# Attention batch 0 whole before the feed-forward part, and half of the k/q transposes by DMA: one change to an attention plus ReGLU kernel

## The chip, the cores and the metric

One core of a Trainium2 chip. The metric is the device time of one execution in microseconds (us), median over repeated runs; 95% intervals use runs in the fast state alone. A "span" is the time from the first to the last instruction of a profiled execution; it is about 1.8 us shorter than the time of the same run. "Clock" is the mean TensorE clock that the profile shows as granted, 1.0 being full speed; below it is the mean over a whole span unless a window is named. In the profiles PE is TensorE (PEld its weight loads), DVE VectorE, ACT ScalarE, POOL GpSimd and SP SyncE, which here only issues DMAs; a q behind a name, as in SPq, stands for the issuing itself. PSUM is the memory that the matmuls write.

## The reference, cut to what matters

```python
# q, k, v: (4 batches, 8 heads, 768 rows, 64); n_sink = 4, window = 128
scores = q @ k.T / 8                              # per batch and head
keep   = (key < 4) | (0 <= query - key < 128)     # 4 sink keys and a sliding window
a      = softmax(where(keep, scores, -1e9))
x      = (a @ v) -> (3072 tokens, 512)
out    = (relu(x @ w_gate) * (x @ w_val)) @ w_out # 512 -> 1536 -> 512
```

The comparison allows bf16 arithmetic. All three weight matrices are fp32 in memory and are cast to bf16 by the DMA that loads them.

## The kernel before: the parts that matter

Two heads are attended together, which I call a unit: 4 units per batch, 16 in all. A unit is a row of stages: `S(0)`, `S(1)`, `S(2)` (scores of three groups of queries, then exp), `T` (transposes of the *next* unit's k and q), and two `norm` (sums and outputs `V`, then the division). The feed-forward part is a row of 96 "chunks": 384 tokens by 128 of the 1536 columns, with gp and vp (four matmuls each), and op matmuls (the output product) some chunks later. Stages are woven between chunks by a plan.

```python
# batch 0 is attended in two halves: units of kind "L" (rows 0 to 375), then "M" (the rest)
U  = [Unit(p, 0, p, "L") for p in range(NP)] + [Unit(NP + p, 0, p, "M") for p in range(NP)]
U += [Unit(2 * NP + (b - 1) * NP + p, b, p, "F") for b in range(1, B) for p in range(NP)]

def T(self, pool, shape, tag, qcopy=nc.scalar.copy):        # every unit: TensorE, then two ScalarE copies
    # ... cut
    for t in range(kn_):
        nc.tensor.transpose(ps[:, t * kp:(t + 1) * kp], self.kn_[0:kp, t, :, :]..., ident[0:kp, 0:kp])
    # ... cut: the same for q, copies PSUM -> kT, qT, and the small copies that place the sink keys (kTs)

# head: four half units, before the first chunk
for p in range(NP):
    U[p].S(0)
    # ... cut: casts and loads
    U[p].S(1)
    if p + 2 < NP:
        U[p + 2].T(*GV)
    # ... cut: loads of weights and casts
    warm(8)                                                  # matmuls on the identity, no useful work
    if p >= 1:
        norm(U[p - 1], 0, ps_gv)
# ... cut
ORDER  = [(0, h, m) for h, m in [(h, m) for h in range(2) for m in range(FM)]]   # token half, then weight column
ORDER += [(b, h, m) for b in range(1, B) for h in range(2) for m in range(FM)]
PLAN = ((0, 0), (2, 0), (10, 19), (23, 43), (47, 67), (71, 89), (72, 90))        # (chunk, stages done by then)
```

The softmax here doesn't subtract the row's maximum and nothing guards it: scores larger than these inputs give would overflow.

## Time and profile before

| | before |
|---|---|
| time, median of 3 runs | 276.72 us (275.81 to 277.87) |
| span of the profiled run | 273.9 us, at clock 0.999 |
| TensorE busy | 259.8 us (95%) |
| first full chunk | 22.8 us |

TensorE is the bound; how that is read, with the page's lines, stands in the prediction below. On the page, the line of all packets and the line of DMA queue q1, which carries all loads that SP (SyncE) issues (columns: packets, megabytes, share of the 16 DMA engines' span):

```profile
DMA packets 46858, 31.20 MB, mean 114 GB/s; under 512 B 28400, under 2 KB 43760, under 8 KB 46832
q1 hardware_dynamic: 40224, 25.93, 34.2%
```

And one row of the table of windows, from 10 to 20 us: busy time and count for each engine, granted clock, DMA share, GB/s.

```profile
10.00:20.00 10.00, 9.87 (x131) 6.61 (x130) 6.63 (x15) 6.57 (x14) 8.29 (x18) 1.00 1.23 234
```

### The profile page before, as it was taken

Reading aid. Unit: us, or ns where it says so; the run is one execution under the profiler, and the core shown is the slowest. Engines: PE = TensorE matmul, PEld = TensorE weight load, DVE = VectorE, ACT = ScalarE, POOL = GpSimd, SP = SyncE. Lnnn points to the kernel's source line nnn. Section 1 sums busy time; section 2 is a strip of 40 time slices with the busy share of each in tenths; the row PEclk is TensorE's granted clock in tenths of the full one; section 3 lists DMA queues with packets and bytes.
Section 4 is the critical chain, followed back from the end, with each engine's and each line's share of the span. In section 5 each row is a group of like instructions: output and inputs, shape, how many; then the busy total and the mean of one; then the engine's idle time right before and its main releaser. Section 6 shows DMA issues by size and latency. Waiting matters only on the chain.

```text
span 273.9 us, 5552 instructions
## 1 busy us (share of the span) xinstructions
PE 259.8 (95%) x2158; PEld 148.4 (54%) x2158; DVE 148.2 (54%) x329; ACT 129.6 (47%) x218; POOL 67.8 (25%) x123
## 2 busy tenths in 40 slices
PE   5997899899989999999999999999999999999994
PEld 4564555555545555555565555555655555555541
DVE  2486355778797755465666646565474722222210
ACT  3743656666646544536435363644535333323321
POOL 7973547653441330030402105000000000000000
PEclk9999999999999999999999999999999999999999
DMA  8999999998465170531707125101101110011122
GB/s 196 260 224 207 246 255 231 254 251 189 114 172 162 54 212 10 159 84 44 209 4 212 41 75 142 38 0 41 38 2 38 41 38 10 28 42 38 38 77 78
DMA packets 46858, 31.20 MB, mean 114 GB/s; under 512 B 28400, under 2 KB 43760, under 8 KB 46832
## 3 DMA queue, kind: packets, MB, share of 16 engines
q1 hardware_dynamic: 40224, 25.93, 34.2%
q0 software_dynamic: 5808, 4.72, 11.0%
q8 instruction: 17, 0.28, 0.4%
q10 hardware_dynamic: 800, 0.20, 0.3%
q14 instruction: 9, 0.07, 0.1%
HBM read 29.26 MB, written 6.29 MB: 130 GB/s over the span
## 4 chain that ended last, share of the span: by engine, by line
PE 84%; DVE 8%; ACT 3%; issue 1%; DMA 1%; POOL 1%; SPq 0%; DVEq 0%; ACTq 0%
PE gp L323 22%; PE op L342 22%; PE vp L329 21%; PE ops L248 7%; PE sps L226 5%; PE sps L221 2%; DVE R L311 2%; PE tkq L180 2%; DVE R L308 2%; PE tkq L183 2%; DVE xT L313 2%; ACT ee L230 2%; DMA stg<-in_q_dram 1%; DVE ee L232 1%; DVE rc L309 1%
## 5 line engine op out<-in xcount | busy, mean ns | idle before, releaser
L326 ACT ACTIVATE gs<-gp 128x384 f32<-128x384 f32 (+2 forms) x96 | 47.3, 493 | 73.2 <-PE gp L323 71.4
L323 PE MATMUL gp<-xT,wg 128*128 128x384 bf16 (+2 forms) x384 | 78.8, 327 | 1.4 <-DVE xT L313 1.4
L331 DVE TENSOR_TENSOR hT<-gs,vp 128x384 bf16<-128x384 f32 (+2 forms) x96 | 52.7, 549 | 49.3 <-PE vp L329 42.1
L329 PE MATMUL vp<-xT,wv 128*128 128x384 bf16 (+2 forms) x384 | 78.1, 326 | 0.0
L342 PE MATMUL op<-wo,hT 128*128 128x512 bf16 x288 | 75.9, 379 | 0.0
L230 ACT ACTIVATE ee<-sps 128x1006 bf16<-128x1006 f32 (+4 forms) x52 | 46.3, 905 | 26.5 <-PE sps L226 26.5
L329 PEld LDWEIGHTS <-wv 128*128 128x128 bf16 x384 | 37.6, 98 | 26.4 <-issue 1.6
L323 PEld LDWEIGHTS <-wg 128*128 128x128 bf16 x384 | 32.5, 98 | 25.2 <-issue 4.3
L342 PEld LDWEIGHTS <-hT 128*128 128x128 bf16 x288 | 28.2, 98 | 25.1
L232 DVE TENSOR_TENSOR ee<-ee,msk 128x1006 bf16<-128x1006 bf16 (+2 forms) x36 | 26.0, 723 | 26.0 <-ACT ee L230 25.8
L153 POOL CAST kn<-stg 128x768 bf16<-128x768 f32 (+2 forms) x20 | 15.4, 768 | 72.9 <-DMA stg<-in_k_dram 48.7
L346 ACT COPY ot<-op 128x512 f32<-128x512 f32 x24 | 14.1, 586 | 21.6 <-PE op L342 21.5
L308 DVE STREAM_TRANSPOSE R<-ops 128x384 f32<-128x384 f32 (+1 forms) x28 | 16.4, 584 | 14.3 <-PE ops L248 14.3
L186 ACT COPY kT<-tkq 128x768 bf16<-128x768 bf16 (+2 forms) x20 | 14.0, 700 | 18.1 <-PE tkq L183 17.9
L157 POOL CAST vn<-stg 128x768 bf16<-128x768 f32 (+2 forms) x20 | 14.4, 720 | 22.7 <-DMA stg<-in_v_dram 16.7
L311 DVE STREAM_TRANSPOSE R<-rc 128x384 f32<-128x384 f32 (+1 forms) x32 | 18.6, 582 | 1.1
L248 PEld LDWEIGHTS <-ones 128*64 128x64 bf16 x280 | 12.1, 109 | 12.3 <-issue 7.4
L313 DVE TENSOR_TENSOR xT<-ops,R 128x384 bf16<-128x384 f32 (+2 forms) x32 | 17.8, 557 | 1.4
L226 PEld LDWEIGHTS <-kT 64*128 64x128 bf16 x136 | 6.6, 93 | 19.2 <-issue 16.8
L248 PE MATMUL ops<-ee,ones 128*64 128x251 bf16 (+9 forms) x256 | 14.3, 238 | 2.2 <-DVE xT L313 1.3
L226 PE MATMUL sps<-qT,kT 64*128 64x251 bf16 (+3 forms) x136 | 15.5, 250 | 0.8 <-ACT qT L188 0.8
L153 POOL CAST qn<-stg 128x768 bf16<-128x768 f32 (+2 forms) x20 | 14.5, 724 | 5.2 <-DMA stg<-in_q_dram 4.8
(53 smaller groups left out, 169.8 us busy)
## 6 DMA issues: line engine op xcount, KB each, us to landing
out_dram<-ot SPq DMA_DIRECT2D x24, 256.0 KB
stg<-in_k_dram SPq DMA_DIRECT2D x12, 384.0 KB
stg<-in_q_dram SPq DMA_DIRECT2D x12, 384.0 KB
stg<-in_v_dram SPq DMA_DIRECT2D x24, 192.0 KB
wg<-in_moe_w_gate_dram POOLq DMA_DIRECT2D x4, 384.0 KB, 9.7
wv<-in_moe_w_val_dram POOLq DMA_DIRECT2D x4, 384.0 KB, 11.8
wo<-in_moe_w_out_dram POOLq DMA_DIRECT2D x3, 512.0 KB, 5.9
stg<-in_k_dram SPq DMA_DIRECT2D x4, 280.0 KB
```

The lines of the kernel that those rows point to most:

```text
L153: cp(dst[0:pp, 0:nn, :, :], self.staging(what)[0:pp, :, :].rearrange("p h (n d) -> p n h d", d=64))
L226: nc.tensor.matmul(out=ps[:, h, c:c + w], lhsT=self.kw(j, r), rhs=qT[s][r, qa:qa + w], start=not biased, stop=True, skip_group_check=True)
L230: nc.scalar.activation(x, ps[:, :, 0:c], Act.Exp, bias=0.0, scale=scale)
L232: nc.vector.tensor_tensor(x, x, bc(msk[:, m0:m0 + c], 2), op=Alu.mult)
L248: nc.tensor.matmul(out=ps[1 - what][64 * h:64 * h + 64, qa - q0:qa - q0 + w], lhsT=self.vn[:, j, h, :] if what else ones[:], rhs=ee[s][:, ...
L311: nc.vector.transpose(r[:, 1, 0:w], bass.AP(a.tensor, a.offset, [a.ap[0], [1, nb], [0, 32]]))
L313: nc.vector.tensor_tensor(xTs[u.b][:, u.p, lo:hi], o[:, lo - c0:hi - c0], r[:, 1, lo - c0:hi - c0], op=Alu.mult)
L323: nc.tensor.matmul(out=gp[:, 0:n], lhsT=wg[:, ko, m * 128:(m + 1) * 128], rhs=x[:, ko, c0:c0 + n], start=ko == 0, stop=ko == KO - 1)
L326: nc.scalar.activation(gs[:, 0:n], gp[:, 0:n], Act.Relu, bias=0.0, scale=1.0)
L329: nc.tensor.matmul(out=vp[:, 0:n], lhsT=wv[:, ko, m * 128:(m + 1) * 128], rhs=x[:, ko, c0:c0 + n], start=ko == 0, stop=ko == KO - 1)
L331: nc.vector.tensor_tensor(hT[:, m, c0:c0 + n], gs[:, 0:n], vp[:, 0:n], op=Alu.mult)
L342: nc.tensor.matmul(out=op, lhsT=hTs[b][:, m, t * 128:(t + 1) * 128], rhs=wo[:, m, :], start=m == 0, stop=m == FM - 1)
```

## The change

The intent: TensorE is the bound, so take work off it and fill its head with real work. (1) Batch 0 is attended in whole units like the others, all of it before the first chunk, so that nothing of it is left behind. (2) The chunks of batch 0 go by weight column first (three columns for both token halves), so that each quarter of the weights is used longer before the next is needed. (3) The k and q of units 8 to 15 (batches 2 and 3) are no longer transposed by TensorE and copied by ScalarE but transposed by DMA inside SBUF. For that their rows are loaded in another order, in runs of 256 bytes instead of 1536.

```diff
+            self.xbar = self.b>1
@@ load_kq
+            if self.xbar:
+                eng.dma_start(out=dst.rearrange("p h (t d) -> p (h t) d", d=64),
+                              in_=src.rearrange("h (t p) d -> p (h t) d", p=128))
+            else:
+                eng.dma_start(out=dst, in_=src.rearrange("h (p n) d -> p h (n d)", n=6))
@@ new
+        def X(self):
+            for x, dst in ((self.kn, kT[self.s]), (self.qn, qT[self.s])):
+                nc.sync.dma_start_transpose(out=dst[:, 0:S].rearrange("d (t r) -> d t r", r=128),
+                                            in_=x[:].rearrange("r t h d -> r (t h d)"))
@@ units
-        U = [Unit(p, 0, p, "L") for p in range(NP)] + [Unit(NP + p, 0, p, "M") for p in range(NP)]
-        U += [Unit(2 * NP + (b - 1) * NP + p, b, p, "F") for b in range(1, B) for p in range(NP)]
+        U = [Unit(i) for i in range(B * NP)]
     ... cut: the head loop with its warm matmuls goes away; all 16 units are stages
@@ stages
+                    if gi == 0 and nxt is not None and nxt.xbar:
+                        nxt.X()
                     u.S(gi)
     ... cut
-                    nxt.T(*AT)
+                    if not nxt.xbar:
+                        nxt.T(not on_array)
+                    nxt.sinkk()
     ... cut: loads of weights by stage; wo part x-5 with unit x = 5, 6, 7, ahead of the casts of unit x+3:
+                elif 5 <= x:
+                    held(x + 3)
+                    if x < 8:
+                        load_wo(x - 5)
@@ order
-        ORDER = [(0, h, m) for h, m in [(h, m) for h in range(2) for m in range(FM)]]
+        ORDER = [(0, h, m) for g in range(0, FM, 3) for h in range(2) for m in range(g, g + 3)]
-        PLAN = ((0, 0), (2, 0), (10, 19), (23, 43), (47, 67), (71, 89), (72, 90))
+        PLAN = ((0, 28), (24, 50), (48, 74), (71, 98))
```

`held(x + 3)` puts the loads of unit x+3 (k, q, then v) into SP's program; `X` of the next unit follows them there, because it belongs to the next stage.

## The prediction

> **What bounds the kernel now.** I read the page's head first, then the slices, the chain that ended last, the waits of TensorE, and last the timeline of TensorE stretch by stretch.
>
> ```profile
> span 273.9 us, 5552 instructions
> PE 259.8 (95%) x2158; PEld 148.4 (54%) x2158; DVE 148.2 (54%) x329; ACT 129.6 (47%) x218; POOL 67.8 (25%) x123
> PE   5997899899989999999999999999999999999994
> DVE  2486355778797755465666646565474722222210
> DMA  8999999998465170531707125101101110011122
> PE 84%; DVE 8%; ACT 3%; issue 1%; DMA 1%; POOL 1%; SPq 0%; DVEq 0%; ACTq 0%
> ```
>
> TensorE (PE) is busy 95% of the span and carries 84% of the chain. The gaps lie at the left: the first third of the slices is where the DMA engines are full too. "Busy" is not "at peak", so I looked at spacing in the quiet middle:
>
> ```profile
> 108.13 0.82 PE L323 MATMUL gp<-xT,wg 128*128 128x384 bf16 x4
> 108.79 0.81 PE L329 MATMUL vp<-xT,wv 128*128 128x384 bf16 x4
> 109.44 1.03 PE L342 MATMUL op<-wo,hT 128*128 128x512 bf16 x4
> 110.30 0.50 PE L180 MATMUL tkq<-ident,kn 128*128 128x128 bf16 x6
> 110.64 0.50 PE L183 MATMUL tkq<-ident,qn 128*128 128x128 bf16 x6
> 110.97 0.81 PE L323 MATMUL gp<-xT,wg 128*128 128x384 bf16 x4
> ```
>
> First number: start. Differences of starts are the true cost: four gp take 0.65 us, four op 0.86, and the twelve transposes of one head pair 110.97 - 110.30 = 0.67 us. No idle is marked on any line: here every matmul counts. After about 92 us there are no waits; the waits are these:
>
> ```profile
> PE gp L323 <- DVE xT L313: 1.4, 1, 1.4
> PE ops L248 <- DVE xT L313: 1.3, 2, 0.7
> PE tkq L180 <- DVE xT L313: 1.1, 2, 0.6
> PE sps L221 <- DVE xT L313: 1.1, 3, 0.4
> ```
>
> Without the gp one, and with two on ScalarE (0.9 and 0.8 us), they make 5.2 us between 23 and 92 us: mostly VectorE, late with the normalisation, holding a PSUM buffer. The start:
>
> ```profile
> 19.63 1.07 PE L370 MATMUL warm<-ident 128*128 128x128 bf16 x16
> 20.76 0.64 PE L323 MATMUL gp<-xT,wg 128*128 128x376 bf16 x3
> 22.77 0.32 PE L323 MATMUL gp<-xT,wg 128*128 128x376 bf16 x1 [1.38 <-DVE xT L313]
> ```
>
> The feed-forward part really starts at 22.8 us. Before that, only the first halves of four head pairs were attended, and warm matmuls (no useful work) fill gaps.
>
> [...] the two 503-column bias matmuls take 1.05 us at 7.78 us and 0.60 us at 13.83. [...]
>
> **The change part by part.** I call one head pair of one batch a unit: 16 units, four per batch.
>
> *Work of TensorE, by differences of starts.* A chunk (gp and vp) 1.30 us, 96 of them: 124.8. An op matmul 0.216, 288: 62.2. A whole unit: scores 0.42 + 0.43 + 0.40 (each with 0.1 us lost at the switch of array shape), sums and outputs 0.92 + 0.82, transposes 0.67: 3.66 us. The later half of a batch 0 unit: 2.9 us (two biased score groups 0.74 each, sums and outputs 0.97, transposes 0.45).
> Books of before: 22.3 us to the first chunk (22.77 less the three gp done earlier), 187.0 feed-forward, 12 x 3.66 = 43.9 for batches 1 to 3, 4 x 2.9 = 11.6, waits 5.2, and 3.8 us from the last matmul (270.1) to the end: 273.8, against a span of 273.9. So the books close, and a change can be priced by its entries.
>
> *DMA transposes.* Units 8 to 15 lose 0.67 us each on TensorE: 5.4 us, all in the stretch without idle, so worth it in full. They also free ScalarE of two copies (0.80 us each) and one use of a PSUM pair per unit; neither is on the path there. Added: two transposes of 192 KB per unit on SP's queue, issued a whole unit ahead; and k and q of these units are loaded in 256-byte runs, at a time when the DMA share is 0.3 to 0.4.
>
> *Batch 0 whole first.* The instruction order shows all four units of batch 0 and the first two score groups of unit 4 ahead of the first chunk. What is left after it: 187.0 + the rest of unit 4 (transposes of unit 5, 0.67, scores 0.40, outputs 0.82: 1.9) + units 5 to 7 (11.0 less the transposes of unit 8: 10.3) + 8 x 2.99 = 23.9: 223.1 us, against 242.5 before. 19.4 us of work has gone from behind the first chunk; the price is a later first chunk. It comes at the later of two times:
> (a) Compute. A biased unit takes TensorE about 5 us (3.66 plus bias columns 2 x 1417 / 2.4 = 1.2), ScalarE 1.01 + 1.01 + 0.87 + 2 x 0.80 = 4.5, VectorE two normalisations of 0.58 + 0.23 + 0.58 + 0.56 = 1.95 and small copies, 4.4. In-order waits between them make that about 5.5 us per unit (estimate). k and q of unit 0 land at about 5 us (0.79 MB at the 270 GB/s of the stretch from 2 to 8 us in before, after 2 us), casts, cold transposes and copies lead to first scores near 8, second unit near 13.6; three units more and the two score groups: 32 us.
> (b) Supply. The order has unit 4's transposes ahead of unit 3's last scores. They need units 0 to 3 (1.19 MB each), k and q of unit 4 (0.79), the first weight quarter (0.79 as bf16) and about half of the second: 6.7 MB. The first 41 us of before moved 9.5 MB, 231 GB/s at a DMA share above 1: 29 us. Two casts (0.83 each) and 4.4 us of TensorE work to the first chunk: 35 us.
> I take 35. Next supply point: unit 5's k and q, 8.3 MB, 36 us, cast by 37.7; two chunks after the first cover it.
>
> *Weight-column-major chunks.* Six chunks use one weight quarter, so quarters are needed 11 us apart; in before, twelve chunks ran through all four. No wait comes from the weights. The output matmuls of batch 0 come later in one lump (63 at the end instead of 36), same number, no cost.
>
> *Waits behind the first chunk.* Before squeezes 24 stages of attention into chunks 10 to 23; VectorE is then over 90% busy and causes most of the 5.2 us. After has 22 stages in 24 chunks: VectorE 0.55 + 0.153 units x 6.6 = 1.56 us per chunk of 1.86. I leave 1.5 us.
>
> Sum: 35 + 223.1 + 1.5 + 3.8 = 263.4 us of span; the timed median lies 2.8 us over before's span: **266 us**.
>
> **Rivals.** *DMA transposes too slow.* [...] For it: nothing here measures it, and SP works in order. [...] About 15%.
> *Supply later than I think.* At 200 GB/s the first chunk comes at 40 us: 271 us, the change near even. For it: GpSimd waited 4.53 us for one v load in before; against: k and q now come in longer runs (1536 bytes) than the halves did. 20%.
> *Cold array.* [...] Likely, and part of my margin.
> *Head hidden better.* If compute and supply both go well, first chunk at 32: 263 us.
>
> **Range and chances.** The centre is 266; I say 266.5, because the rivals mostly point up. The first chunk between 31.5 and 40 and slack waits give 262 to 272; the transposes stretch the upper end: 261 to 277. Faster by over 2% means below 271.2: 0.71. Within 2%: 0.18. Slower: 0.11.
>
> **What would show it.** Right: first gp at 33 to 38 us; TensorE without marked idle from there on; twelve transposes gone after about 90 us, a unit then 3.0 us; last op group 66 long. Wrong: transposes of unit 4 waiting on GpSimd's cast later than 33 us; kTs copies or scores that wait for a DMA into kT or qT once per unit (then the DMA transposes bound the kernel); TensorE waits on VectorE of more than 3 us in the first 24 chunks; pairs of bias matmuls at 1 us instead of 0.6 late in the head.

Three of its figures, as before's timeline shows them. Four gp of 384 columns take 0.65 us and four op of 512 columns 0.86 us by their starts, so 2.36 and 2.38 columns per ns: the 2.4 by which (a) divides. From an op group to scores, which have another array shape, the starts lie 0.96 us apart (106.85 to 107.81 us), to transposes of the same shape 0.86 (109.44 to 110.30): the 0.1 us at a switch. And the four transposes of a half unit's k take 0.50 us at 4.47 us and 0.34 at 12.26: "cold" in (a) means such slow first ones.

## The result, and the profile after

| | before | after |
|---|---|---|
| time, median | 276.26 us (275.64 to 277.87, 4 runs) | 267.62 us (264.36 to 269.0, 4 runs) |
| repeated later, 5 rounds | 276.26 us (11 runs) | 266.18 us (264.34 to 267.28, 6 runs) |
| span of the profiled run | 273.9 us | 262.6 us (265.2 in the repeat) |
| first gp | 22.8 us (first whole chunk) | 31.06 us |

The ratio after to before is 0.9639 [0.9536, 0.9742] the first time and 0.9628 [0.959, 0.9665] in the repeat: 3.7% faster. All ratios here are the mean time of one kernel's fast runs over the mean of the other's of the same rounds, so not quite the ratio of the medians.

The same lines of the page as the prediction shows of before, here of the kernel after:

```profile
span 262.6 us, 5141 instructions
PE 249.7 (95%) x1992; PEld 138.6 (53%) x1992; DVE 146.3 (56%) x318; ACT 115.5 (44%) x186; POOL 63.2 (24%) x102
PE   3989899999978999999999999999999999999994
DMA  7999999996989691919378591311011001111132
q1 hardware_dynamic: 71216, 28.12, 46.8%
PE 79%; DVE 8%; DMA 7%; ACT 2%; SPq 2%; issue 1%; POOL 1%; DVEq 0%; POOLq 0%; ACTq 0%
```

TensorE is still busy 95% of the span; it has 10.1 us less to do (249.7 against 259.8). The share of 95% hides two new things. There is a dent at slices 12 and 13 (72 to 85 us), where TensorE drops to 7 and 8 tenths. And DMA, 1% of the chain before, is now 7%. The queue q1 carries 31,000 more packets for 8% more bytes, at a third more of the engines' time. The list of TensorE's waits (total, times, longest) behind the first chunk names the dent:

```profile
PE op L294 <- DMA wo<-in_moe_w_out_dram: 2.7, 1, 2.7
PE vp L281 <- DVE R L260: 0.5, 1, 0.5
```

The timeline of all engines tells how that wait came about, read from the bottom up (start, duration, engine, source line, what; in brackets the idle before it and what ended it):

```profile
31.06 0.81 PE L275 MATMUL gp<-xT,wg 128*128 128x384 bf16 x4 [0.26 <-DVE xT L265]
...
62.12 6.64 SPq L120 DMA_DIRECT2D stg<-in_v_dram  x2
...
69.94 1.32 SPq L137 DMA_TRANSPOSE kT<-kn  x1
...
70.38 1.05 POOL L127 CAST qn<-stg 128x768 bf16<-128x768 f32 x1 [5.10 <-PE vp L281]
...
72.94 0.75 DVE L159 COPY kTs<-kT 128x372 bf16<-128x372 bf16 x1 [1.75 <-DMA kT<-kn]
...
73.26 0.74 POOL L214 DMA_DIRECT2D wo<-in_moe_w_out_dram  x1
...
79.94 0.38 PE L294 MATMUL op<-wo,hT 128*128 128x512 bf16 x1 [2.72 <-DMA wo<-in_moe_w_out_dram]
```

TensorE waited 2.72 us at 79.94 for the third part of the output weights. GpSimd issued that load only at 73.26, because in its program it stands behind the casts of unit 9's k, q and v, and the cast of q ran only at 70.38, 9.0 us after q's load was issued (61.36). The profile puts the 5.10 us idle before that cast down to TensorE, but TensorE had last read this buffer for unit 6's transposes at about 46.5 us, so what it waited for must be q's load; in the run with the sooner first chunk below, the profile names that load at the same step. The queue was full meanwhile (DMA share 1.10 from 62 to 69 us): SP needed 6.64 us to issue two v loads that take 1.16 us in a quieter queue (shown in an experiment below). The share alone does not set this time: the same issue took 1.05 us at 12.99, where the share is 1.16 (mean from 10 to 20 us). The first DMA transpose, issued at 69.94, released VectorE's copy at 72.94: 3.0 us from issue to use.

The last op group is 66 long, from 244.44 to 258.85 us, as foretold, and 3.75 us later the span ends.

The head was faster than predicted. The same row of windows as of before, 10 to 20 us:

```profile
10.00:20.00 10.00, 8.83 (x126) 5.53 (x124) 7.45 (x15) 7.57 (x10) 8.22 (x14) 1.00 1.16 306
```

The engines are about as full (1.16 against 1.23) but move 306 GB/s instead of 234, which I put down to batch 0's k and q now being loaded in whole units and so in longer runs (1536 bytes, where before's first halves have 1024 and 768). That is an estimate: no run isolates this, and the mix of loads in the two windows differs. The transposes of unit 4, which by the prediction's supply estimate (29 us and two casts) had to wait until about 31 us, started at 26.47 with no marked wait.

The repeat of after had two kinds of fast runs: three at clock 1.0 with 264.3 to 265.4 us, and three at clock 0.994 with 266.9 to 267.3 us. Its profiled run was one of the latter. Two rows of its windows, behind the same wait for wo (2.84 us there, ended at 80.9 us):

```profile
82.00:84.00 2.00, 1.78 (x8) 0.93 (x7) 0.98 (x2) 1.05 (x2) 1.04 (x2) 0.57 1.34 222
84.00:86.00 2.00, 2.00 (x22) 1.12 (x20) 0.26 (x1) 0.59 (x1) 0.56 (x2) 0.57 1.13 92
```

The granted clock (third number from the right) is 0.57 for these four microseconds, which costs 4 x 0.43 = 1.7 us (an estimate from the clock; the vp group at 82.21 took 1.39 us instead of 0.81). That is 0.006 of the span, so this one dip is the whole of the mean clock of 0.994. In the profiled run with the 2.72 us wait it stayed 1.00 there. So a wait of 2.84 us was followed by a dip in one run and one of 2.72 us by none in another. That the dip follows the wait is shown; that the wait caused it is not, as no run here isolates it. (Four of the six runs of the kernel with long runs, below, were granted 0.991 to 0.994 too, though its profiled run has no such wait; so not every low clock need come from it.)

### The profile page after: what moved, and what is told of

Same layout as the page of the kernel before. It is cut to its first block, busy times and chain, and to the rows that moved or that the text cites.

```text
span 262.6 us, 5141 instructions
## 1 busy us (share of the span) xinstructions
PE 249.7 (95%) x1992; PEld 138.6 (53%) x1992; DVE 146.3 (56%) x318; ACT 115.5 (44%) x186; POOL 63.2 (24%) x102
## 2 busy tenths in 40 slices
DMA packets 77318, 33.54 MB, mean 128 GB/s; under 512 B 64496, under 2 KB 74224, under 8 KB 77296
## 3 DMA queue, kind: packets, MB, share of 16 engines
q1 hardware_dynamic: 71216, 28.12, 46.8%
## 4 chain that ended last, share of the span: by engine, by line
PE 79%; DVE 8%; DMA 7%; ACT 2%; SPq 2%; issue 1%; POOL 1%; DVEq 0%; POOLq 0%; ACTq 0%
PE gp L275 23%; PE op L294 23%; PE vp L281 21%; PE ops L201 6%; PE sps L179 4%; DMA wo<-in_moe_w_out_dram 3%; DMA stg<-in_v_dram 2%; DVE R L263 2%; DVE xT L265 2%; DMA stg<-in_k_dram 2%; DVE R L260 2%; SPq L120 1%; DVE kTs L159 1%; DVE kTs L160 1%; ACT kT L153 1%
## 5 line engine op out<-in xcount | busy, mean ns | idle before, releaser
L278 ACT ACTIVATE gs<-gp 128x384 f32<-128x384 f32 x96 | 47.1, 490 | 72.6 <-PE gp L275 71.9
L275 PE MATMUL gp<-xT,wg 128*128 128x384 bf16 x384 | 78.7, 328 | 0.3 <-DVE xT L265 0.3
L281 PE MATMUL vp<-xT,wv 128*128 128x384 bf16 x384 | 78.1, 326 | 0.5 <-DVE R L260 0.5
L283 DVE TENSOR_TENSOR hT<-gs,vp 128x384 bf16<-128x384 f32 x96 | 52.7, 551 | 42.2 <-PE vp L281 40.0
L183 ACT ACTIVATE ee<-sps 128x1006 bf16<-128x1006 f32 (+2 forms) x48 | 46.2, 965 | 38.9 <-PE sps L179 38.9
L130 POOL CAST vn<-stg 128x768 bf16<-128x768 f32 x16 | 14.1, 884 | 21.7 <-DMA stg<-in_v_dram 14.4
L263 DVE STREAM_TRANSPOSE R<-rc 128x384 f32<-128x384 f32 x32 | 18.5, 579 | 1.1
L265 DVE TENSOR_TENSOR xT<-ops,R 128x384 bf16<-128x384 f32 x32 | 17.8, 557 | 1.7
L201 PE MATMUL ops<-ee,vn 128*64 128x255 bf16 (+8 forms) x288 | 15.5, 233 | 0.4 <-DVE xT L265 0.3
L179 PE MATMUL sps<-qT,kT 64*128 64x251 bf16 (+2 forms) x128 | 14.9, 255 | 0.1
```

The costliest lines, as they stand in the source:

```text
L179: nc.tensor.matmul(out=ps[:, h, c:c + w], lhsT=self.kw(j, r), rhs=qT[s][r, qa:qa + w], start=not self.biased, stop=True, skip_group_check= ...
L183: nc.scalar.activation(x, ps[:, :, 0:c], Act.Exp, bias=0.0, scale=scale)
L201: nc.tensor.matmul(out=ps[1 - what][64 * h:64 * h + 64, qa - q0:qa - q0 + w], lhsT=self.vn[:, j, h, :] if what else ones[:], rhs=ee[s][:, ...
L263: nc.vector.transpose(r[:, 1, 0:w], bass.AP(a.tensor, a.offset, [a.ap[0], [1, nb], [0, 32]]))
L265: nc.vector.tensor_tensor(xTs[u.b][:, u.p, c0:c0 + w], o[:, 0:w], r[:, 1, 0:w], op=Alu.mult)
L275: nc.tensor.matmul(out=gp[:, 0:n], lhsT=wg[:, ko, m * 128:(m + 1) * 128], rhs=x[:, ko, c0:c0 + n], start=ko == 0, stop=ko == KO - 1)
```

## The experiments

My theory after the result: the DMA transposes are worth the 5.4 us of TensorE work that they remove, and batch 0 whole is worth some 8 us; but in this arrangement the two do not add, because loads in 256-byte runs and the long programs of SP and GpSimd make the wo load late, and 3 to 4 us are given back in the middle. Rivals: the transposes themselves wait somewhere and are worth less than 5.4 us; or it is the place of the wo load alone; or the first chunk's time rules all.

| kernel | median us | ratio to before [95%] | profiled span, clock |
|---|---|---|---|
| after, repeated | 266.18 | 0.9628 [0.959, 0.9665] | 265.2, 0.994 |
| all transposes on TensorE | 268.05 | 0.9692 [0.9664, 0.972] | 265.5, 0.999 |
| before, with DMA transposes | 270.14 | 0.9777 [0.9749, 0.9805] | 268.5, 1.0 |
| wo issued sooner | 265.46 | 0.9605 [0.9576, 0.9635] | 261.5, 1.0 |
| long runs again | 264.92 | 0.9556 [0.9514, 0.9599] | 260.5, 0.997 |
| chunks token-half first | 270.69 | 0.9716 [0.9664, 0.9768] | 267.6, 0.985 |
| each DMA transpose twice | 272.74 | 0.9873 [0.9839, 0.9907] | 270.9, 0.987 |
| DMA transposes from batch 1 | 284.72 | 1.0297 [1.0249, 1.0345] | 282.8, 0.97 |
| v loads behind transposes | 262.20 | 0.9488 [0.9445, 0.9531] | 260.7, 0.998 |
| first chunk sooner | 269.99 | 0.9769 [0.974, 0.9799] | 269.4, 0.981 |
| both of the last two | 262.62 | 0.9506 [0.9471, 0.9542] | 259.7, 0.998 |
| the same, wo first | 262.57 | 0.9497 [0.946, 0.9534] | 261.1, 1.0 |

Before had medians of 276.25 to 276.53 us beside them. They ran in four groups on three chips, so across groups I compare ratios. Medians are over all runs; the ratios leave out the slow ones (one of the four first runs of after, 269.0 us; one in "all transposes on TensorE"; two each in "long runs again" and "chunks token-half first"). All of them ran on one core, so "slow" means only more than 1.5% above the fastest run of the same kernel.

### The kernel after once more

No edit.

> The changed kernel unaltered, to have it beside the others on one chip. Expected ratio to the kernel before: 0.965, span 262 to 266 us, first feed-forward matmul at 31 us, one wait of about 2.7 us of an op matmul for wo near 80 us.

Measured: ratio 0.9628, and the two groups of runs described above. The result holds. The two profiled runs, one of each kind, differ by 2.6 us of span: 1.7 us are the clock dip by the estimate above, and most of the rest is a wait of 0.99 us for GpSimd's cast of q at 35.69 us that the first profile doesn't have.

### All transposes on TensorE

```diff
-            self.xbar = self.b>1
+            self.xbar = False
```

> All transposes back on TensorE, batch 0 whole first and the chunk order kept. The books of the prediction: plus 5.4 us on TensorE against the changed kernel. Refined theory: k and q of batches 2 and 3 come in 1536-byte runs again, so the wait for wo (2.7 us) goes; net plus 2.5 to 3 us, about 1%, ratio to before 0.975. Rival (the transposes lie in idle time anyway): no change against the changed kernel but for the wo wait, ratio 0.955.

Measured: 268.05 us, ratio 0.9692; span 265.5 against 262.6 for after, so 2.9 us longer, and 1.9 us in the medians. The wait for wo is gone, and q1's share falls back to 33.2%. So the reordering of batch 0 alone takes 3.1%, 8.4 us by spans (273.9 - 265.5); the transposes beside it add only 2 to 3 us in this kernel. The second figure is what had to be explained: 5.4 us of TensorE work had gone.

### The kernel before, with DMA transposes for batches 2 and 3

```diff
@@ load_kq
+                if self.xbar:
+                    eng.dma_start(out=dst.rearrange("p h (t d) -> p (h t) d", d=64),
+                                  in_=x[b, 2 * p:2 * p + 2].rearrange("h (t p) d -> p (h t) d", p=128))
+                    continue
@@ X() as in the change, and in T():
+            if self.xbar:
+                ...the two kTs copies alone...
+                return
@@ stages
+                    if gi == 0 and nxt is not None and nxt.xbar:
+                        nxt.X()
```

> The kernel before (halves of batch 0, its own chunk order) with one part of the change alone: k and q of batches 2 and 3 loaded in 256-byte runs and transposed by DMA. Theory (each unit's 0.67 us on TensorE is worth it in full, as no debt arises this late in that kernel): minus 5.4 us, ratio 0.980. Rival (the new loads and transposes cost waits as they do in the changed kernel): minus 2.5 to 3 us, ratio 0.99.

Measured: 270.14 us, ratio 0.9777; span 268.5 against 273.9, 5.4 us less. That is 8 units x 0.67 us; that it fits to the tenth is chance, since the medians differ by 6.1 us (276.25 - 270.14). VectorE's copies of kTs waited for the DMA 0.7 us in all, two times. So in a kernel that never waits for wo, the DMA transposes are worth at least what they take off TensorE. The rival that they are worth less by their nature falls.

### wo issued sooner

```diff
-                    if x < 8:
-                        load_wo(x - 5)
+                    if x == 5:
+                        load_wo(0)
+                    elif x == 6:
+                        load_wo(1)
+                        load_wo(2)
```

> The third part of wo is asked for one unit earlier (right behind the second). Theory (the wo wait near 80 us is new idle time on the path): it vanishes, 2.5 us faster than the changed kernel, ratio 0.955. Rival (another wait takes its place, since the DMA queues are full there, or the wait only hides a later one): no change.

Measured: 265.46 us, ratio 0.9605 against 0.9628: 0.6 us less, within the intervals of both; by spans 1.1 us less than the first profile of after. The wait for wo is gone, but the timeline of all engines shows what came in its place:

```profile
70.02 3.32 SPq L137 DMA_TRANSPOSE kT<-kn  x1
...
76.15 0.31 DVE L159 COPY kTs<-kT 128x372 bf16<-128x372 bf16 x1 [4.42 <-DMA kT<-kn]
...
77.05 0.81 PE L275 MATMUL gp<-xT,wg 128*128 128x384 bf16 x4 [1.14 <-DVE hT L283]
```

The first transpose took 6.1 us from issue to the copy, beside busier DMA engines (share 1.21 from 70 to 72 us and 1.58 from 72 to 74, against 0.78 and 0.60 in after); that this is the reason was not isolated. VectorE, which works in order, stood there for 4.42 us with the hT products behind it, and TensorE waited 1.14 us for those. The rival was largely right: the wait moved. This suggests that what is short is not wo's place but the queue.

### Long runs again

The loads of batches 2 and 3 go back to 1536-byte runs, the transposes stay. The rows then land in other positions, so the result is wrong. (The comparison let it pass; with inputs of scale 0.1 the scores are small, so this says little for the kernel.)

```diff
-            if self.xbar:
-                eng.dma_start(out=dst.rearrange("p h (t d) -> p (h t) d", d=64),
-                              in_=src.rearrange("h (t p) d -> p (h t) d", p=128))
-            else:
-                eng.dma_start(out=dst, in_=src.rearrange("h (p n) d -> p h (n d)", n=6))
+            eng.dma_start(out=dst, in_=src.rearrange("h (p n) d -> p h (n d)", n=6))
```

> Wrong result on purpose: k and q of batches 2 and 3 loaded in 1536-byte runs (token order wrong), DMA transposes kept. Theory (256-byte runs fill the DMA queues and so make wo late): wo wait gone, DMA busy share of the SP queue down from 46.8% to near 36%, 2.5 us faster, ratio 0.955. Rival (wo is late through GpSimd's program order alone): wait and time stay.

Measured: 264.92 us, ratio 0.9556; span 260.5, and no wait for wo. The page's queue line:

```profile
q1 hardware_dynamic: 50736, 28.12, 41.4%
```

It carries the same 28.12 MB as after in 20,480 fewer packets, and takes 41.4% of the engines' span instead of 46.8%. (I had put it at about 36%; the transposes themselves take more of the queue than I had thought: with all transposes on TensorE it was 33.2%.) So short runs cost some 0.7% of the time, 2 us, by the ratios. This size is weak: the intervals overlap, the ratio leaves out two runs at 267.01 and 267.35 us, about as long as the longest that counts as fast in after (267.28), and the medians over all runs differ by 1.3 us. That the wait for wo goes is plain. So is that the same bytes, loaded in 256-byte runs, took 5.4 points more of q1's share here.

### Chunks of batch 0 token-half first

```diff
-        ORDER = [(0, h, m) for g in range(0, FM, 3) for h in range(2) for m in range(g, g + 3)]
+        ORDER = [(0, h, m) for h in range(2) for m in range(FM)]
...
-            for _ in range(min(3, len(f2))):
+            for _ in range(min(3, len(f2)) if ci > 20 else 0):
```

The second edit keeps the op matmuls of batch 0 where they were, so that in the main only the order of the chunks differs.

> Changed kernel, but the first 24 chunks run through all weight columns for the first half of the tokens, then for the second (output matmuls start at the same chunk as in the changed kernel). Theory (weight quarters are asked for so late that column order is needed): TensorE waits for the third and fourth quarter at chunks 6 and 9, near 42 to 52 us, 4 to 8 us in all, ratio 0.98 to 0.99. Rival (order is immaterial): ratio 0.963.

Measured: ratio 0.9716, 0.9% over the repeat of after. That is less than I had expected, though the direction was right. The timeline of TensorE names the cause:

```profile
46.15 0.82 PE L275 MATMUL gp<-xT,wg 128*128 128x384 bf16 x4 [2.36 <-DMA wg<-in_moe_w_gate_dram]
48.88 1.46 PE L281 MATMUL vp<-xT,wv 128*128 128x384 bf16 x4 [1.90 <-DMA wv<-in_moe_w_val_dram]
```

In the token-half order the weights are late by 4.3 us in two waits, with a clock dip after them (0.50 from 48 to 52 us; mean 0.985). The vp group above runs 1.46 us instead of 0.81. The net loss is 2.4 us (0.9% of 276) by the two fast runs of four, 4.5 us by the medians. This kernel has no wait for wo (2.7 us in after), which offsets a part; the sizes are not closed. So weight-column-major order removes these two waits; without it the change would still be 2.8% faster than before.

### Each DMA transpose twice

```diff
-            for x, dst in ((self.kn, kT[self.s]), (self.qn, qT[self.s])):
+            for x, dst in ((self.kn, kT[self.s]), (self.kn, kT[self.s]), (self.qn, qT[self.s]), (self.qn, qT[self.s])):
```

> Changed kernel with every DMA transpose issued twice (same result). Theory (transposes have slack behind the first unit): 0 to 2 us, all of it at the first of them near 70 us; ratio up to 0.97. Rival (the transposes or SP's queue are the bound of batches 2 and 3): 3 us or more for each of eight units, ratio above 1.03.

Measured: 272.74 us, ratio 0.9873, between the two expectations (up to 0.97, or over 1.03). VectorE's kTs copies waited for the DMA 20.6 us in seven waits, the longest 6.4, and scores waited 5.7 us for qT. In the quiet middle:

```profile
117.51 5.70 SPq L137 DMA_TRANSPOSE kT<-kn  x2
...
124.75 0.29 DVE L159 COPY kTs<-kT 128x372 bf16<-128x372 bf16 x1 [2.48 <-DMA kT<-kn]
```

Two transposes into one tile hold SP for 5.70 us, where one takes 1.2. Why the second is issued so late was not shown; my guess is that it waits for the first to land, as both write the same tile. So this doubles the time to landing (7.2 us from first issue to copy, against 3.0 in after), not only the work of the queue, and overstates the cost. What it does show is that the slack is small. One landing more per tensor already puts VectorE and TensorE into waits that cost 2.5% of before's time (0.9873 - 0.9628).

### DMA transposes from batch 1 on

```diff
-            self.xbar = self.b>1
+            self.xbar = self.b>0
```

> Changed kernel with the DMA transposes from batch 1 on (units 4 to 15 instead of 8 to 15). The books alone: four units more lose 0.67 us each on TensorE, minus 2.7 us, ratio 0.953. Theory (the DMA queues are full until 60 us, 256-byte runs and SP's order make the first of these transposes late): TensorE or VectorE waits for kT or qT by DMA before the first chunk and in the first 24 chunks, 5 us or more, ratio 0.97 to 0.99.

Measured: 284.72 us, ratio 1.0297, slower than before. Against after I had the direction, not the size. The timeline of all engines where unit 4's first transposes are issued and used:

```profile
35.59 1.32 SPq L137 DMA_TRANSPOSE kT<-kn  x1
...
37.02 1.22 SPq L137 DMA_TRANSPOSE qT<-qn  x1
...
40.03 0.39 PE L179 MATMUL sps<-qT,kT 64*128 64x255 bf16 x2 [12.66 <-DMA qT<-qn]
```

TensorE stood still for 12.66 us. The casts of unit 4's k and q were done at 24.2 and 28.3 us, but SP issued their transposes only at 35.59 and 37.02: before them in SP's program stood the loads of a later unit, one of which (q at 27.18) took 5.45 us to issue in a full queue (DMA share 1.04 from 26 to 41 us). q's transpose thus waited 8.7 us for its turn, and from its issue to the scores it was then 3.0 us. So it was late more by its place in an in-order program than by its duration. Further waits come on top: 7.8 us for hT and 3.7 us for wo, and the mean clock is 0.97. This supports that the change stops at batch 2, and it points to the next experiment.

### v loads behind the transposes

```diff
@@ held(): k and q only
-                load(x)
+                U[x].load_kq("k", nc.sync)
+                U[x].load_kq("q", nc.sync)
@@ stage s(0), behind nxt.X()
+                    if gi == 0 and x >= 6 and at(x + 2) is not None:
+                        at(x + 2).load_v(nc.sync)
@@ stage t()
-                    if x < 8:
-                        load_wo(x - 5)
+                    if x == 5:
+                        load_wo(0)
+                        load_wo(1)
+                    elif x == 6:
+                        load_wo(2)
+                if x >= 6 and at(x + 2) is not None:
+                    casts(at(x + 2), "v")
                 if at(x + 3) is not None:
-                    casts(at(x + 3), "kqv")
+                    casts(at(x + 3), "kqv" if x < 5 else "kq")
```

k and q of a unit are needed a unit before its v. So SP issues v's loads after the transposes, GpSimd casts v a unit later, and wo goes out sooner, ahead of casts that wait.

> Changed kernel with wo asked for earlier (two parts with unit 5, the third with unit 6) and the v loads of batches 2 and 3 queued on SP behind the DMA transposes of the unit before instead of ahead of them. Theory (what is left of waits behind the first chunk is SP's order: the first DMA transpose stands behind v loads in a full queue): no wait for wo, none of VectorE for kT, span 259 us at full clock, ratio 0.95. Rival (waits only move again, as with wo alone): 261 us or more, ratio 0.96.

Measured: 262.20 us (260.62 to 264.02), ratio 0.9488 [0.9445, 0.9531], 5.1% faster than before and about 1.5% faster than after (0.9488 / 0.9628, across two chips). SP's part of the timeline of all engines:

```profile
67.04 2.17 SPq L137 DMA_TRANSPOSE kT<-kn  x1
69.31 1.22 SPq L137 DMA_TRANSPOSE qT<-qn  x1
70.59 1.16 SPq L120 DMA_DIRECT2D stg<-in_v_dram  x2
```

The transposes go 2.9 us earlier than in after, and the same two v loads, issued when the queue is emptier (DMA share 0.73 from 70 to 72 us, against 1.10 from 62 to 69 us in after), take 1.16 us of SP instead of 6.64. From 52 to 100 us no wait of TensorE is marked, and VectorE waits for no kT. Bytes and packets are those of after (77318, 33.54 MB): same work, other order. This version beats both kernels. The edit bundles the order of v and that of wo; wo's place alone brought 0.6 us by the ratios in the wo run above, so most is probably due to v's place. But v's place alone was not run, and the two may not add up. That no wait for wo is left says nothing of v: the third part of wo is issued at 58.49 here instead of 73.26.

### First chunk sooner

```diff
-        PLAN = ((0, 28), (24, 50), (48, 74), (71, 98))
+        PLAN = ((0, 25), (24, 50), (48, 74), (71, 98))
```

Three stages of attention fewer stand before the first chunk.

> Changed kernel with the first chunk three stages sooner (right after unit 3's first half is normalised; unit 4's first scores and unit 3's second half follow between chunks). Theory of the books (work only moves from before the first chunk to behind it; only idle time of TensorE counts): first chunk near 29.5 us instead of 31, total within 1 us of the changed kernel, ratio 0.96 to 0.965. Rival (the lateness of the first chunk is itself the cost of attending batch 0 whole first): 1.5 us faster, ratio 0.957.

Measured: 269.99 us, ratio 0.9769, 1.4% slower than after; neither expectation held. The first gp started at 28.97 us instead of 31.06, though its fourth matmul waited until 31.05 for a normalisation. But the wait for wo grew to 5.46 us: its third part was issued at 75.53 instead of 73.26, behind a cast of q that ran at 72.73 instead of 70.38, while the op matmuls came to it only 0.4 us sooner (76.26 instead of 76.62). The windows around the wait:

```profile
78.00:82.00 4.00, 0.00 (x0) 0.00 (x0) 0.00 (x0) 0.00 (x0) 0.00 (x0) 0.71 1.16 201
86.00:90.00 4.00, 3.46 (x19) 1.64 (x21) 1.45 (x3) 1.08 (x2) 1.87 (x4) 0.51 0.52 88
```

For four microseconds none of the five engines has anything to do before that DMA lands, and the clock then stays near half until 90 us: over the 8 us from 82 to 90 the mean is 0.51, by estimate 8 x 0.49 = 3.9 us lost on top. The test was confounded by wo, so I ran it again on top of the better order.

### Both: v loads behind the transposes, and the first chunk sooner

```diff
 (the v order above, and)
-        PLAN = ((0, 28), (24, 50), (48, 74), (71, 98))
+        PLAN = ((0, 25), (24, 50), (48, 74), (71, 98))
```

> The v loads behind the transposes, and the first chunk three stages sooner. If the loss of the run with the sooner first chunk alone was only the wait for wo (5.5 us) that this order takes away, the 2 us gained at the head are kept: first gp near 29 us, no wait for wo above 1 us, span near 259 us against 260.7, ratio to before 0.942. If the sooner start merely shifts attention work into the chunks behind it, where VectorE and the transposed copies of batch 1 can't keep pace, marked waits of TensorE on VectorE and GpSimd come to 2 us or more in the first 24 chunks, and the span stays at 260.5 us or above, ratio 0.949 or more.

Measured: 262.62 us, ratio 0.9506 [0.9471, 0.9542], against 0.9488 with the first chunk at 31.17: the same. The wait for wo is gone, as expected, which fits that this wait and its clock made the run before slow. The 2 us at the head were not kept, though:

```profile
27.33 0.66 PE L275 MATMUL gp<-xT,wg 128*128 128x384 bf16 x3
...
29.21 0.32 PE L275 MATMUL gp<-xT,wg 128*128 128x384 bf16 x1 [1.22 <-DVE xT L265]
```

TensorE now waits for VectorE's normalisations, twice, 2.5 us in all, and the three stages that were left out come later. The second expectation was right in its mechanism and its ratio: work that moves behind the first chunk is still work. Its bound for the span, 260.5 us or above, was missed by the profiled run (259.7, the fastest of the six).

### The same, with all of wo first

```diff
                     if x == 5:
                         load_wo(0)
                         load_wo(1)
-                    elif x == 6:
                         load_wo(2)
```

> As the run before, with all three parts of wo issued after unit 5's transposes. If wo still holds the run before by more than 1 us, this one is faster by that; if not, the same within 0.4 us, or up to 1 us slower because the casts of unit 8 on GpSimd and the loads start behind 1.6 MB more of weights.

Measured: 262.57 us, ratio 0.9497, the same within 0.1%. wo holds nothing any more, and one can stop there.

## Why the prediction was right, point by point

The prediction was 266.5 us with a range of 261 to 277 and 71% for "faster by over 2%". Measured: 267.62 and 266.18 us, 3.7% faster. The span was predicted at 263.4; the first profile has 262.6 and the second 265.2. (The first was of the fastest run, 264.36 us, so the medians lie further above it than the 2.8 us that I had added.) The total is right; two of its terms were wrong in opposite directions, 4 us too much for the head and about 2 us too little behind it, and that they partly cancel is luck.

- **DMA transposes, 5.4 us: right.** The kernel before with this part alone lost 5.4 us of span (6.1 us by medians). The rival that they are too slow fell (its chance was an estimate, as before has no DMA transpose): in after the first 128x768 transpose took 3.0 us from issue to use, most take 1.2 to 1.3 us of SP (1.94 at the most), and VectorE's copies of kTs waited for one once, not once per unit.
- **Batch 0 whole first, supply (b), first chunk at 35 us: wrong by 4 us.** The first gp came at 31.06, outside the 33 to 38 us that I had named as the sign of being right, and by the compute side (a), which I had put at 32; this is the rival "head hidden better". The mis-sized term is the supply: q of unit 4 was cast at 23.53 without a marked wait, so it had landed by then, where I had 29 us. The rate was 231 GB/s, taken from before's first 41 us, where after moved 263 in its first 24 us (306 from 10 to 20); and I had counted half of the second weight quarter, whose load was issued only at 21.29. I had named the longer runs as a reason, and did not put it into the number. The rhythm of 5.5 us per biased unit was right in the mean: the first scores of units 0 to 4 start at 7.13, 12.53, 18.75, 23.64 and 28.96, so 4.9 to 6.2 us apart, 5.46 on average.
- **Work behind the first chunk, 223.1 us: right within about 1.5 us.** 31.06 + 223.1 + 3.75 = 257.9; the span is 262.6; marked waits behind the start of the first chunk are 2.72 + 0.46 = 3.2 us, which leaves 1.5 us that I can't assign.
- **Waits behind the first chunk, 1.5 us by VectorE: wrong in kind and size.** VectorE cost 0.46 us. The rest, 2.7 us, was the wait for wo, which no rival named, and with which the sign "TensorE without marked idle from there on" failed; in the profiled run of the repeat the clock behind it took another 1.7 us by estimate, and six of the ten runs have a mean clock of 0.994 or less. The reading of before was off, too: in chunks 10 to 23 (50.8 to 91.5 us) VectorE was busy for 33.9 of 40.7 us, 83% and not over 90%, and the waits for it there come to 2.4 us, not most of the 5.2. I had noted the 256-byte runs and dismissed them, because I took the DMA share to be 0.3 to 0.4 at that time; the loads of units 9 and 10, though (issued from 60.90 and 73.75), fall between 60 and 80 us, beside the last weights, where the share in after is 0.85.
- **Column-major chunks, no wait from the weights: right**, and worth more than I wrote. The token-half order would bring 4.3 us of such waits.
- **Cold array: it did not come.** Its sign was bias pairs at 1 us instead of 0.6 late in the head, where most of the warm matmuls are gone. The pair takes 1.05 us at 7.13 us and 0.60 at 12.53, and none after that takes longer than 0.60. (The granted clock reads 1.00 from 7 to 8 us, so the profile's clock does not show the slow pairs at the start; the durations do.)
- **The books.** Reordering alone: 8.4 us of span. Transposes alone: 5.4 us. Sum 13.8 us, and 273.9 - 13.8 = 260.1. After shows 262.6 or 265.2; the version with v's loads behind the transposes shows 260.7. By the ratios it is 0.9692 x 0.9777 = 0.948, against 0.9488 for that version. So the two parts add up when the queue is put in order, and after gave back 2.5 to 5 us of their sum. That the giving back comes from the queue around 60 to 80 us rests on three runs: with long runs, and with all transposes on TensorE, the wait for wo goes, while with wo alone issued sooner the wait moves to a DMA transpose. The order of v and wo together brings the sum back; how much of that is v alone is not shown.

What stays open: how much the clock dip costs apart from the wait (no run has one without the other in a controlled way), what the place of v's loads is worth alone, and the 1.5 us that the account above leaves over.

## What to carry to other kernels

When work moves from the bound engine to DMA, price not only the transfer but its place in the issuing engine's in-order program (with transposes from batch 1, q's transpose waited 8.7 us for its turn on SP and took 3.0 us from issue to use), and look for the next load in a full queue that somebody will need: here it was a weight load that had nothing to do with the change. Issue first what is needed first (k and q and their transposes before v), and a saving that was half lost can come in full, as here, with the same bytes and packets. Starting the main part sooner was worth nothing by itself, since the work left out had to be done later, beside the engine that is the limit.
